# Sliding-window attention and token MLP, two layers: key-offset products summed in groups of 16, softmax pinned ahead of PV, one layer's norms shared between two engines

## The chip, the core and the metric

The kernel runs on one core of one Trainium2 chip. The core has TensorE (PE, matmuls), VectorE (DVE), ScalarE (ACT), GpSimd (POOL) and SyncE (SP, here only a queue that issues DMAs); each works through its own instruction queue, and semaphores tie the queues together. The metric is the device time of one execution in microseconds.

## The reference

Two attention layers and two token-mixing MLPs, applied in turn to x of 2048 tokens by 1024 features, all in bf16:

```python
for _ in range(2):
    x = x + A(layernorm(x))      # attention
    x = x + B(layernorm(x))      # MLP over tokens

def A(x):                        # 32 heads of 32
    q, k, v = split(x @ wqkv)
    # token s sees tokens s, s-2, ..., s-14 (8 offsets, dilation 2)
    logits = q[s] . k[s - 2w] / sqrt(32), w = 0..7; -1e9 where s - 2w < 0
    o = softmax(logits) weighted sum of v[s - 2w]
    return o @ wo

def B(x):
    h = layernorm(x)
    u = gelu(h.T @ w1 + b1)      # over tokens: 1024 x 2048 @ 2048 x 3584
    return (u @ w2 + b2).T
```

## The kernel before

**Two classes.** Because the dilation is 2, even and odd tokens never meet in the attention. The kernel treats them as two classes c = 0 and 1 of 1024 tokens each. Within a class, eight neighbouring tokens form a window. Features lie on the partitions: a feature tile `dt` is 128 features (4 heads), and four feature tiles make one unit n of the attention: n = 0 and 1 are class 0, n = 2 and 3 class 1.

**QK** (`qk`, L436 to L449). For each feature tile and each parity `par` of the key offset, DVE multiplies q with four shifted copies of k in one instruction of 128 x 4096 elements into a buffer T (L444). Two buffers of tag "T" are shared by T, by the PV products `pr` and by a copy of w2. TensorE then sums the 32 features of each head: eight matmuls (L449) with a 0/1 matrix `sel` of 128 x 32 columns, one for each of the eight token blocks, into a PSUM tile `sc`. The eight use four column strips of the array. Half a feature tile (one `par`) is thus one DVE instruction and one group of eight matmuls.

**Softmax** (`softmax_front` L453, `softmax_back` L463). ACT copies `sc` to L (L455), DVE finds and subtracts the maximum (L456 to L460), ACT takes the exp (L461), DVE sums, takes the reciprocal and multiplies into Pb (L466 to L470). POOL's queue writes Pb to DRAM (pd, L473) and reads it back, spread over the partitions of each head, as two halves pb (L487); there are two pb buffers, one for each half.

**PV** (`pv`, L489 to L511). For each feature tile and half `hf`, DVE multiplies pb with shifted v (two L505), adds the eight offsets in three steps (L509 twice, L511) and writes oT.

**Output projection** (`out_proj`, L611). oT times wo (L631) per token tile i and half n of the columns, plus the residual on DVE (L652, with the row sums, or L655), then a layer norm to h2. With the flag `on_act` the norm runs on ACT (L219 to L233: sums, square, Ln, Exp, scale), otherwise on DVE (bn_stats L202, L204, and L228) with Ln and Exp on ACT. Class 0 takes ACT for all eight tiles in both layers; class 1 alternates, and multiplies six of the eight feature tiles of its first three token tiles early.

**MLP.** `gemm1` (L682) multiplies h2 with w1 into g, 14 blocks of g; for the first 12 blocks class 0's part is computed ahead of time ("partials") and class 1's added later (L693, L694). `gemm2_tile` (L706) multiplies g with w2, adds bias and residual on DVE (L711), stores, normalises to `hb` and transposes by DMA to hT, the input of the next layer's projections (`project`, L412).

**What sets the order.** The attention's generator `stream` (L514) is the lead. Each step yields its engine, its planned cost, what it waits for, what it makes ready, and a lag. `weave` (L755) keeps one planned clock for PE and one for DVE, and while the lead would leave PE waiting it pulls PE work from the fills: the second class's tiles, v projections ahead, class 0's output projection ("out0") and partials. "out0" is also pulled when DVE has planned more than OUT0_GAP of work and PE is less than AHEAD in front of DVE. The order in which instructions are recorded gives a priority, and a scheduler of the language then orders each engine's queue by its own costs. It may put instructions of PV between those of the softmax, and split or merge neighbouring groups. Only the first tiles of layer 0 are written out by hand.

**Buffers that the change touches.** g_raw is 14 tiles of SBUF that hold g; the first six are also the landing place of x, the last eight that of class 1's v. PSUM has six banks for `ps` and two for `sc`. The pool "wb" has five buffers for wv, wo, w1 and w2 pieces, "x2" four for residual rows and `hb`.

Of the kernel before, what the change touches and what calls it, by code (L numbers as in the profile page):

```python
# [11 lines left out]
ALU = mybir.AluOpType  # L12
FP32 = mybir.dt.float32
BF16 = mybir.dt.bfloat16

P = 128
H = 32
DH = 32
W = 8
# [7 lines left out]
def kernel(  # L27
# [39 lines left out]
    PB_LAG = 12.0  # L67
    PDW = 4 * SB * W * TB + 512
    OUT0_GAP = 7.0
    AHEAD = 10.0  # L70
    assert D == H * DH and W == 8 and SC == 1024 and HD * KD == H and SB * CH == 32
    scale = float(DH) ** -0.5

# [7 lines left out]
    pers = pool("pers", 1)  # L81
    wqp = pool("wqp", 3)
    wbp = pool("wbp", 5)
    tpl = pool("tpl", 2)
# [6 lines left out]
    class at:  # L91
# [8 lines left out]
        def __exit__(self, *a):  # L100
            self.c[0] = tc.cur_priority
            tc.cur_priority = self.old

    tc.cur_priority = 10_000_000
    top = [1_000_000]
# [30 lines left out]
    sel = const.tile([P, SB * DQ, 32], BF16, name="sel")  # L136
# [28 lines left out]
    L = pers.tile([P, W, TB], FP32, name="L")  # L165
    m4 = pers.tile([P, 4, TB], FP32, name="m4")
    Pb = pers.tile([P, W, TB], BF16, name="Pb")
    g_raw = [pers.tile([P, 2 * KW if n >= NFB - KD else GF * D], BF16, name=f"g{n}") for n in range(NFB)]
    g = [t[:, 0:GF * D].rearrange("p (f d) -> p f d", d=D) for t in g_raw]
    v_g = [t[:].rearrange("p (r k) -> p r k", k=KW) for t in g_raw[NFB - KD:]]  # L170
# [181 lines left out]
    class Attn:  # L352

        def __init__(self, li, hT, early):
            self.li, self.hT, self.early = li, hT, early
            self.oT = [[None] * KD for _ in range(DIL)]
            self.wts = {}
            self.pbs = {}

        def v_of(self, c, dt):  # L360
            return v_g[dt] if c else v_t[dt % 2]
# [72 lines left out]
        def qk(self, n, dq):  # L434
            c, dt = n // NCQ, (n % NCQ) * DQ + dq
            if dq == 0:  # L436
                self.sc = pssp.tile([P, 2, 4, TB], FP32, name="sc", tag="sc")
            q, k = self.q_of(c, dt), self.k_of(c, dt)
            for par in range(2):
                yield "dve", 2.2, [("ready", 0, dt), ("ready", 1, dt)], [("free", x, dt % 2) for x in range(2)] if par and not self.apart(c, dt) else [], 0.0, 0.6 * bool(n)  # L440
                if n == 0:
                    yield "pe", 0.6, [], [], 0.0
                T = tpl.tile([P, 4, SC], BF16, name="T", tag="T")
                nc.vector.tensor_tensor(out=T[:], in0=q.unsqueeze(1).to_broadcast([P, 4, SC]),  # L444
                                        in1=window(k, par, 2, [(2, 4), (1, SC)]), op=ALU.mult)
                for sb in range(SB):
                    for gr in range(4):
                        b = SB * gr + sb
                        nc.tensor.matmul(self.sc[32 * gr:32 * gr + 32, par], lhsT=sel[:, sb * DQ + dq, :],  # L449
                                         rhs=T[:, :, b * TB:(b + 1) * TB],  # L450
                                         start=(dq == 0 and sb == 0), stop=(dq == DQ - 1 and sb == SB - 1))

        def softmax_front(self):  # L453
            yield "dve", 4.5, [], ["exp"], 1.2, 0.0
# [8 lines left out]
        def softmax_back(self, n):  # L463
            yield "dve", 3.0, ["exp"], [("pb", n, 0)], PB_LAG, 0.0
            yield "dve", 0.0, [], [("pb", n, 1)], PB_LAG + 6.0, 0.0
            nc.vector.tensor_tensor(out=m4[:], in0=L[:, 0:4, :], in1=L[:, 4:8, :], op=ALU.add)  # L466
            nc.vector.tensor_tensor(out=m4[:, 0:2, :], in0=m4[:, 0:2, :], in1=m4[:, 2:4, :], op=ALU.add)
            nc.vector.tensor_tensor(out=m4[:, 0, :], in0=m4[:, 0, :], in1=m4[:, 1, :], op=ALU.add)
            nc.vector.reciprocal(out=m4[:, 1, :], in_=m4[:, 0, :])
            nc.vector.tensor_tensor(out=Pb[:], in0=L[:], in1=m4[:, 1:2, :].to_broadcast([P, W, TB]), op=ALU.mult)  # L470
            base = self.pd(n)[0, 0]
            dst = bass.AP(base.tensor, base.offset, [(W * TB, 4 * SB), (PDW, CH), (1, W * TB)])
            nc.gpsimd.dma_start(out=dst, in_=Pb[:].rearrange("p u t -> p (u t)"))  # L473
            self.spread(n)
# [14 lines left out]
        def pv(self, n, half, hf, dqs=(0, 1)):  # L489


            c = n // NCQ
            for dq in (2 * half + x for x in dqs):
                dt = (n % NCQ) * DQ + dq
                if hf == 0 and c and dt < 2 * DIL:
                    self.oT[c][dt] = v_t[dt // 2][:, dt % 2, PADK + 8:PADK + 8 + SC]
                elif hf == 0:
                    self.oT[c][dt] = otp.tile([P, SC], BF16, name="oT", tag="oT")[:]
                waits = [("pb", n, hf)] + ([] if c else [("ready", 2, dt)])
                yield "dve", 4.7, waits, [("free", 2, dt % 2), "oT", ("oT", half)] if hf else [], 0.0, 0.0  # L500
                pb = self.pbs[(n, hf)]
                pr = tpl.tile([P, 4, W, TB], BF16, name="pr", tag="T")
                for par in range(2):
                    u = slice(4 * par, 4 * par + 4)
                    nc.vector.tensor_tensor(out=pr[:, :, u, :], in0=pb[:, :, u, :],  # L505
                                            in1=window(self.v_of(c, dt), par, 2 + hf * HT, [(TB, 4), (2, 4), (1, TB)]),
                                            op=ALU.mult)
                for wd in (4, 2):
                    nc.vector.tensor_tensor(out=pr[:, :, 0:wd, :], in0=pr[:, :, 0:wd, :], in1=pr[:, :, wd:2 * wd, :],  # L509
                                            op=ALU.add)  # L510
                nc.vector.tensor_tensor(out=self.oT[c][dt][:, hf * HT:(hf + 1) * HT].rearrange("p (b t) -> p b t", t=TB),  # L511
                                        in0=pr[:, :, 0, :], in1=pr[:, :, 1, :], op=ALU.add)
# [95 lines left out]
                nc.sync.dma_start(out=self.tiles[-1][:], in_=src)  # L608
            return self.tiles.pop(0)

    def out_proj(at_, c, res, dst, h2, on_act):  # L611

        early = 0 if on_act else 3
        if early:
            yield "pe", 1.28 * early * NDC, [("oT", 0), ("less", "oT", -12.0)], [], 0.0
        dst_v = rows(dst)
# [10 lines left out]
        def multiply(i, n, kts):  # L627
            if (i, n) not in banks:
                banks[(i, n)] = bank()
            for kt in kts:  # L630
                nc.tensor.matmul(banks[(i, n)][:], lhsT=at_.oT[c][kt][:, i * P:(i + 1) * P],  # L631
                                 rhs=wo_t[n][kt // 4][:, kt % 4, :], start=(kt == 0), stop=(kt == KD - 1))

        def kts(i):
            return range(KD - 2 if i < early else 0, KD)

        for i in range(early):
            for n in range(NDC):
                multiply(i, n, range(KD - 2))
        xrs = Rows([res[i] for i in range(NT)], 2)  # L640
        for i in range(NT):
            if early:
                yield "pe", 0.43 * len(kts(i)), ["oT"], [], 3.6
                on_act = i % 2 == 0
            xn = xrs.take()
            s1 = st("s1", [P, NDC]) if on_act else None
            for n in range(NDC):
                cols = slice(n * 512, (n + 1) * 512)
                multiply(i, n, kts(i))
                ps = banks.pop((i, n))  # L650
                if on_act:
                    nc.vector.scalar_tensor_tensor(out=xn[:, cols], in0=ps[:], scalar=1.0, in1=xn[:, cols], op0=ALU.mult,  # L652
                                                   op1=ALU.add, accum_out=s1[:, n:n + 1])
                else:
                    nc.vector.tensor_tensor(out=xn[:, cols], in0=ps[:], in1=xn[:, cols], op=ALU.add)  # L655
            nc.gpsimd.dma_start(out=dst_v[i], in_=xn[:])
# [167 lines left out]
    for li in range(2):  # L824
# [96 lines left out]
```

## Time and profile before

| | us |
|---|---|
| median of 3 runs | 1294.18 (1294.08 to 1295.04) |
| the profiled execution | 1291.79 |
| its span in the trace | 1290.0 |
| PE busy | 1263.8 (98%) |
| DVE busy | 680.5 (53%) |
| ACT busy | 502.7 (39%) |
| L449, `sel` matmuls, x512 | 38.5 |
| L444, T, x64 | 144.5 |
| L505, PV products, x128 | 152.2 |

The table's engine and line figures are those of the one profiled execution. Matmuls overlap in the array, so the busy time of PE's groups is a sum of overlapping durations within the group's line and not the time that they hold the array; a stretch of PE is read from its starts. "Idle before" and "waited for" name what ended a pause. TensorE's granted clock is full throughout. Layer 0's attention runs to about 304 us, its MLP to about 560, layer 1's attention to about 925, and the rest is the last MLP.

### The profile page before, as it was taken

The page shows a single profiled execution, that of the slowest core. Times are in us where ns is not written, and L with a number is a line of the kernel's source. Part 1 is how long each engine was busy: PE and PEld are TensorE (multiplying, and loading weights), DVE is VectorE, ACT ScalarE, POOL GpSimd, SP SyncE. Part 2 cuts the span into 40 slices and gives each one's busy share as a digit, 9 for nine tenths or more (in the row PEclk, how much of TensorE's full clock was granted, in tenths as well). Part 3 has the DMA queues.
Part 4 walks back from the last instruction along what each step waited for, and adds up shares of the span by engine and source line. Part 5 has one row for each costly group of instructions (what it writes and reads, how often), then busy time and mean ns, then how long its engine had stood idle before and what let it go on. Part 6 is the DMA issues. An engine that isn't in the chain of part 4 may idle for free. (4 is left out here: it accounts for less than half of the span.)

```text
span 1290.0 us, 15498 instructions
## 1 busy us (share of the span) xinstructions
PE 1263.8 (98%) x6163; PEld 574.5 (45%) x6284; DVE 680.5 (53%) x861; ACT 502.7 (39%) x836; POOL 60.8 (5%) x166
## 2 busy tenths in 40 slices
PE   8999999999999999999999999999999999999999
PEld 4344444444444444444444444444444444444444
DVE  6879899989013422335895734978920233011011
ACT  6845446635324533325414435484343344000000
POOL 3000001001000000000000000010000000000000
PEclk9999999999999999999999999999999999999999
DMA  9852436563422289953646652349252222334331
GB/s 253 188 122 87 118 106 167 163 153 109 136 82 82 61 221 301 298 147 94 153 125 179 164 135 84 72 142 226 67 179 76 72 82 73 121 121 136 103 112 53
DMA packets 217817, 173.01 MB, mean 134 GB/s; under 512 B 32080, under 2 KB 198352, under 8 KB 215696
## 3 DMA queue, kind: packets, MB, share of 16 engines
q1 hardware_dynamic: 206768, 126.11, 36.5%
q0 software_dynamic: 9248, 37.51, 10.3%
q10 hardware_dynamic: 1728, 8.39, 1.7%
q8 instruction: 49, 0.80, 0.3%
q14 instruction: 24, 0.20, 0.0%
HBM read 139.47 MB, written 26.21 MB: 128 GB/s over the span
## 5 line engine op out<-in xcount | busy, mean ns | idle before, releaser
L682 PE MATMUL ps<-h,w 128*128 128x512 bf16 x1756 | 386.7, 379 | 4.8 <-ACT h L233 2.1
L706 PE MATMUL ps<-g,w 128*128 128x512 bf16 (+1 forms) x1785 | 388.0, 376 | 3.4 <-ACT v L419 1.6
L706 PEld LDWEIGHTS <-w 128*128 128x128 bf16 x1820 | 177.4, 98 | 212.8 <-issue 6.0
L682 PEld LDWEIGHTS <-w 128*128 128x128 bf16 x1792 | 175.1, 98 | 215.8 <-issue 4.5
L412 PE MATMUL ps<-hT,wq 128*128 128x512 bf16 (+1 forms) x1085 | 241.4, 374 | 3.6 <-DVE xr L711 0.9
L693 DVE TENSOR_TENSOR tmp<-ps,g 128x512 f32<-128x512 f32 x96 | 66.4, 692 | 211.3 <-PE ps L682 206.0
L444 DVE TENSOR_TENSOR T<-q,k 128x4096 bf16<-128x4096 bf16 x60 | 135.6, 2286 | 63.2 <-ACT q L416 52.5
L711 DVE SCALAR_TENSOR_TENSOR xr<-ps,b_sb,xr 128x512 bf16<-128x512 f32 (+1 forms) x65 | 45.6, 737 | 230.7 <-PE ps L706 188.7
L412 PEld LDWEIGHTS <-wq 128*128 128x128 bf16 x1112 | 108.3, 100 | 131.6 <-issue 13.4
L509 DVE TENSOR_TENSOR pr<-pr 128x2048 bf16<-128x2048 bf16 (+1 forms) x128 | 119.2, 946 | 0.2
L694 ACT ACTIVATE g<-tmp,b_sb 128x512 bf16<-128x512 f32 x96 | 69.3, 721 | 93.3 <-DVE tmp L693 92.9
L412 PE MATMUL ps<-hT,wv 128*128 128x512 bf16 x436 | 100.6, 380 | 1.0 <-issue 0.5
L631 PE MATMUL ps<-wo,oT 128*128 128x512 bf16 x377 | 89.1, 379 | 2.7 <-DMA wo<-in_A_wo_dram 2.4
L688 ACT CAST g<-ps 128x512 bf16<-128x512 f32 x96 | 55.1, 589 | 91.5 <-PE ps L682 85.8
L419 ACT CAST k<-ps 128x1024 bf16<-128x1024 f32 x60 | 60.7, 1015 | 72.6 <-PE ps L412 71.2
L505 DVE TENSOR_TENSOR pr<-pb,v 128x2048 bf16<-128x2048 bf16 x64 | 75.9, 1215 | 21.1 <-DMA pb<-pd 11.0
L505 DVE TENSOR_TENSOR pr<-pb,g 128x2048 bf16<-128x2048 bf16 x64 | 76.3, 1215 | 11.0 <-DMA pb<-pd 11.0
L412 PEld LDWEIGHTS <-wv 128*128 128x128 bf16 x448 | 48.6, 112 | 50.5 <-issue 7.2
L631 PEld LDWEIGHTS <-oT 128*128 128x128 bf16 x384 | 37.2, 98 | 48.7 <-issue 4.6
L416 ACT CAST q<-ps 128x512 bf16<-128x512 f32 x60 | 34.8, 583 | 47.4 <-PE ps L412 47.4
L419 ACT CAST g<-ps 128x1024 bf16<-128x1024 f32 x36 | 36.6, 1016 | 40.7 <-PE ps L412 40.7
L737 ACT COPY odd<-w 128x896 bf16<-128x896 bf16 x32 | 30.0, 938 | 56.0 <-DMA w<-in_B_w_dram 55.8
(91 smaller groups left out, 606.1 us busy)
## 6 DMA issues: line engine op xcount, KB each, us to landing
w<-in_B_w_dram SPq DMA_DIRECT2D x56, 512.0 KB, 4.3
w<-in_B_w_dram SPq DMA_DIRECT2D x64, 448.0 KB, 3.8
wq<-in_A_wqkv_dram SPq DMA_DIRECT2D x38, 512.0 KB, 4.1
pb<-pd POOLq DMA_DIRECT2D x16, 1024.0 KB, 10.0
wo<-in_A_wo_dram SPq DMA_DIRECT2D x16, 512.0 KB, 4.0
xa<-xr POOLq DMA_DIRECT2D x32, 256.0 KB, 3.4
xr<-xa SPq DMA_DIRECT2D x32, 256.0 KB, 3.6
wv<-in_A_wqkv_dram SPq DMA_DIRECT2D x14, 512.0 KB, 5.7
```

Of the source, the lines that this page charges most:

```text
L412: nc.tensor.matmul(ps[:, lo:hi], lhsT=cols, rhs=self.hT[c][hf][:, kt, lo:hi], start=(kt == 0), stop=(kt == KD - 1))
L419: nc.scalar.copy(out=window(buf, 0, PADK + hf * HT, [(KW + 1, 2), (1, HT)]), in_=ps[:].unsqueeze(1).to_broadcast([P, 2, HT]))
L444: nc.vector.tensor_tensor(out=T[:], in0=q.unsqueeze(1).to_broadcast([P, 4, SC]), in1=window(k, par, 2, [(2, 4), (1, SC)]), op=ALU.mult)
L505: nc.vector.tensor_tensor(out=pr[:, :, u, :], in0=pb[:, :, u, :], in1=window(self.v_of(c, dt), par, 2 + hf * HT, [(TB, 4), (2, 4), (1, TB) ...
L509: nc.vector.tensor_tensor(out=pr[:, :, 0:wd, :], in0=pr[:, :, 0:wd, :], in1=pr[:, :, wd:2 * wd, :], op=ALU.add)
L631: nc.tensor.matmul(banks[(i, n)][:], lhsT=at_.oT[c][kt][:, i * P:(i + 1) * P], rhs=wo_t[n][kt // 4][:, kt % 4, :], start=(kt == 0), stop=( ...
L682: nc.tensor.matmul(ps[:], lhsT=wt[c][:, i, fl * P:(fl + 1) * P], rhs=h2[c][i // 4][:, i % 4, dc * 512:(dc + 1) * 512], start=(k == 0), sto ...
L688: nc.scalar.copy(out=gs, in_=ps[:])
L693: nc.vector.tensor_tensor(out=tmp[:], in0=ps[:], in1=gs, op=ALU.add)
L694: nc.scalar.activation(out=gs, in_=tmp[:], func=ACT.Gelu_apprx_tanh, bias=b1_sb[:, ft:ft + 1])
L706: nc.tensor.matmul(ps[:, 0:xc.stop - xc.start], lhsT=w2t(ft, c), rhs=g[ft // GF][:, ft % GF, xc], start=(ft == 0), stop=(ft == FT - 1))
L711: nc.vector.scalar_tensor_tensor(out=xo[:, xc], in0=ps[:, 0:xc.stop - xc.start], scalar=b2_sb[:, i, c:c + 1], in1=xo[:, xc], op0=ALU.add, ...
```

## The change

- `qk`: except in layer 0's n = 0, both T of a feature tile are made first and then summed in one group of 16 matmuls. A dependency of the first of the 16 on the second multiply, and a chain through the 16, keep the group together. The plan's step is 4.5 of DVE and then 1.1 of PE, where it was twice 2.2 and 0.6.
- `t_buf`: for layer 0's n = 1 and 2, T lies in g's first six tiles, which are now three double tiles `g_two`; elsewhere T keeps the two shared buffers.
- `self.prior`: each QK multiply, in the joined steps, is ordered behind the one before it or behind the last Pb, and each PV product is ordered behind the last QK multiply or Pb recorded before it, by dependencies of order on the same engine. So the softmax's DVE instructions up to Pb stand ahead of the PV products that are recorded after it.
- `out_proj`: `early` and `every` take the place of `on_act`. Class 0 keeps ACT for all tiles in layer 0 and alternates ACT and DVE in layer 1. Without `early`, the first column half of tiles 0 and 1 is multiplied before the rest.
- AHEAD is 5.0 instead of 10.0.

```diff
-    AHEAD = 10.0
+    AHEAD = 5.0
...
+    def follow(inst, other, how):
+        tc.add_manual_dep(inst.ins, other.ins.name, mybir.DependencyInfo(how, mybir.DependencyReason.DATA), reason="follow")
...
-    g_raw = [pers.tile([P, 2 * KW if n >= NFB - KD else GF * D], BF16, name=f"g{n}") for n in range(NFB)]
+    g_two = [pers.tile([P, 2 * GF * D], BF16, name=f"gg{n}") for n in range((NFB - KD) // 2)]
+    g_raw = [t[:, h * GF * D:(h + 1) * GF * D] for t in g_two for h in range(2)]
+    g_raw += [pers.tile([P, 2 * KW], BF16, name=f"g{n}")[:] for n in range(NFB - KD, NFB)]
...
+            ready = [("ready", 0, dt), ("ready", 1, dt)]
+            free = [] if self.apart(c, dt) else [("free", x, dt % 2) for x in range(2)]
+            joined = n > 0 or self.li > 0
+            if joined:
+                yield "dve", 4.5, ready, free, 0.0, 1.1
+            Ts = []
             for par in range(2):
-                yield "dve", 2.2, [("ready", 0, dt), ("ready", 1, dt)], [("free", x, dt % 2) for x in range(2)] if par and not self.apart(c, dt) else [], 0.0, 0.6 * bool(n)
-                if n == 0:
+                if not joined:
+                    yield "dve", 2.2, ready, free if par else [], 0.0, 0.0
                     yield "pe", 0.6, [], [], 0.0
-                T = tpl.tile([P, 4, SC], BF16, name="T", tag="T")
-                nc.vector.tensor_tensor(out=T[:], in0=q.unsqueeze(1).to_broadcast([P, 4, SC]),
-                                        in1=window(k, par, 2, [(2, 4), (1, SC)]), op=ALU.mult)
-                for sb in range(SB):
-                    for gr in range(4):
-                        b = SB * gr + sb
-                        nc.tensor.matmul(self.sc[32 * gr:32 * gr + 32, par], lhsT=sel[:, sb * DQ + dq, :],
-                                         rhs=T[:, :, b * TB:(b + 1) * TB],
-                                         start=(dq == 0 and sb == 0), stop=(dq == DQ - 1 and sb == SB - 1))
+                T = self.t_buf(n, dq, par)
+                mult = nc.vector.tensor_tensor(out=T, in0=q.unsqueeze(1).to_broadcast([P, 4, SC]),
+                                               in1=window(k, par, 2, [(2, 4), (1, SC)]), op=ALU.mult)
+                Ts.append(T)
+                if joined and self.prior:
+                    follow(mult, self.prior, mybir.DependencyClass.NoSync)
+                self.prior = mult
+                if not joined:
+                    self.qk_sum(dq, par, T)
+            if joined:
+                mms = self.qk_sum(dq, 0, Ts[0]) + self.qk_sum(dq, 1, Ts[1])
+                follow(mms[0], mult, mybir.DependencyClass.Sync)
+                for x, y in zip(mms[1:], mms):
+                    follow(x, y, mybir.DependencyClass.NoSync)
+
+        def t_buf(self, n, dq, par):
+            if self.li == 0 and 0 < n < 3:
+                return g_two[(2 * (n * DQ + dq) + par) % len(g_two)][:].rearrange("p (u t) -> p u t", u=4)
+            return tpl.tile([P, 4, SC], BF16, name="T", tag="T")[:]
...
-            nc.vector.tensor_tensor(out=Pb[:], in0=L[:], in1=m4[:, 1:2, :].to_broadcast([P, W, TB]), op=ALU.mult)
+            self.prior = nc.vector.tensor_tensor(out=Pb[:], in0=L[:], in1=m4[:, 1:2, :].to_broadcast([P, W, TB]),
+                                                 op=ALU.mult)
...
-                    nc.vector.tensor_tensor(out=pr[:, :, u, :], in0=pb[:, :, u, :],
-                                            in1=window(self.v_of(c, dt), par, 2 + hf * HT, [(TB, 4), (2, 4), (1, TB)]),
-                                            op=ALU.mult)
+                    mult = nc.vector.tensor_tensor(out=pr[:, :, u, :], in0=pb[:, :, u, :],
+                                                   in1=window(self.v_of(c, dt), par, 2 + hf * HT, [(TB, 4), (2, 4), (1, TB)]),
+                                                   op=ALU.mult)
+                    follow(mult, self.prior, mybir.DependencyClass.NoSync)
...
-    def out_proj(at_, c, res, dst, h2, on_act):
-
-        early = 0 if on_act else 3
+    def out_proj(at_, c, res, dst, h2, early=0, every=1):
+
...
+        if not early:
+            for i in range(2):
+                multiply(i, 0, range(KD))
         for i in range(NT):
             if early:
                 yield "pe", 0.43 * len(kts(i)), ["oT"], [], 3.6
-                on_act = i % 2 == 0
+            on_act = i % every == 0
...
-                multiply(i, n, kts(i))
+                if early or (i, n) not in banks:
+                    multiply(i, n, kts(i))
...
-        lead = chain(at_.stream(opening() if first else None), out_proj(at_, 1, res[1], xa[li][1], h2, on_act=False))
+        lead = chain(at_.stream(opening() if first else None), out_proj(at_, 1, res[1], xa[li][1], h2, early=3, every=2))
...
-                     "out0": out_proj(at_, 0, res[0], xa[li][0], h2, on_act=True),
+                     "out0": out_proj(at_, 0, res[0], xa[li][0], h2, every=li + 1),
```

More of the change, by code (lines that the diff above doesn't have):

```diff
@@ L167 @@
     Pb = pers.tile([P, W, TB], BF16, name="Pb")
-    g_raw = [pers.tile([P, 2 * KW if n >= NFB - KD else GF * D], BF16, name=f"g{n}") for n in range(NFB)]
+    g_two = [pers.tile([P, 2 * GF * D], BF16, name=f"gg{n}") for n in range((NFB - KD) // 2)]
+    g_raw = [t[:, h * GF * D:(h + 1) * GF * D] for t in g_two for h in range(2)]
+    g_raw += [pers.tile([P, 2 * KW], BF16, name=f"g{n}")[:] for n in range(NFB - KD, NFB)]
     g = [t[:, 0:GF * D].rearrange("p (f d) -> p f d", d=D) for t in g_raw]
-    v_g = [t[:].rearrange("p (r k) -> p r k", k=KW) for t in g_raw[NFB - KD:]]
+    v_g = [t.rearrange("p (r k) -> p r k", k=KW) for t in g_raw[NFB - KD:]]
     xa = [[dram.tile([SC, D], BF16, name=f"xa{li}{c}") for c in range(DIL)] for li in range(2)]
@@ L358, in __init__ @@
             self.pbs = {}
+            self.prior = None
         def v_of(self, c, dt):
@@ new lines, in t_buf, with qk_sum @@
+        def t_buf(self, n, dq, par):
+            if self.li == 0 and 0 < n < 3:
+                return g_two[(2 * (n * DQ + dq) + par) % len(g_two)][:].rearrange("p (u t) -> p u t", u=4)
+            return tpl.tile([P, 4, SC], BF16, name="T", tag="T")[:]
+        def qk_sum(self, dq, par, T):
+            mms = []
+            for sb in range(SB):
+                for gr in range(4):
+                    b = SB * gr + sb
+                    mms.append(nc.tensor.matmul(self.sc[32 * gr:32 * gr + 32, par], lhsT=sel[:, sb * DQ + dq, :],
+                                                rhs=T[:, :, b * TB:(b + 1) * TB],
+                                                start=(dq == 0 and sb == 0), stop=(dq == DQ - 1 and sb == SB - 1)))
+            return mms
```

## The prediction

> **What bounds the kernel now.** I read the page's busy times first, then the list of TensorE's own waits, then the timelines of PE and VectorE (DVE) around those waits and around the small `sel` matmuls (L449).
>
> ```profile
> span 1290.0 us, 15498 instructions
> ## 1 busy us (share of the span) xinstructions
> PE 1263.8 (98%) x6163; PEld 574.5 (45%) x6284; DVE 680.5 (53%) x861; ACT 502.7 (39%) x836; POOL 60.8 (5%) x166
> ```
>
> ```profile
> PE sc L449 <- DVE T L444: 3.6, 3, 1.9
> PE ps L631 <- DMA wo<-in_A_wo_dram: 2.4, 2, 1.7
> PE ps L682 <- ACT h L233: 2.1, 3, 1.0
> PE ps L706 <- ACT v L419: 1.6, 2, 0.9
> PE ps L412 <- DVE xr L711: 0.9, 1, 0.9
> ```
>
> TensorE is the bound from end to end; nothing else comes near. A change can pay in two ways only: less PE time, or fewer pauses of PE. In the PE timeline the pauses after the first 60 us are 1.85 (at 104.9, T), 1.71 (191.1, wo), 0.72 (244.8, h), 0.29 (629.6, wq), 0.92 (674.4, xr), 0.87 and 0.72 (710.3 and 711.4, v), 0.26 (754.7, hT), 0.65 (842.1, wo), 1.04 and 0.36 (873.1 and 880.3, h) and 0.81 us (948.2, w): 10.2 us in all, 4.3 in layer 0 and 5.9 in layer 1. That is the most that better ordering can give.
>
> The other source is the small matmuls. PE's timeline in layer 1:
>
> ```profile
> 765.19 0.62 PE L449 MATMUL sc<-T,sel 128*32 128x512 bf16 x8
> 765.74 1.92 PE L412 MATMUL ps<-hT,wv 128*128 128x512 bf16 x8
> 767.59 0.62 PE L449 MATMUL sc<-T,sel 128*32 128x512 bf16 x8
> 768.14 0.41 PE L412 MATMUL ps<-hT,wv 128*128 128x512 bf16 x1
> 768.48 0.62 PE L449 MATMUL sc<-T,sel 128*32 128x512 bf16 x8
> ...
> 849.96 0.61 PE L449 MATMUL sc<-T,sel 128*32 128x512 bf16 x8
> 850.51 3.63 PE L631 MATMUL ps<-wo,oT 128*128 128x512 bf16 x16
> 854.06 1.05 PE L449 MATMUL sc<-T,sel 128*32 128x512 bf16 x16
> 855.04 2.12 PE L631 MATMUL ps<-wo,oT 128*128 128x512 bf16 x8
> 857.13 0.61 PE L449 MATMUL sc<-T,sel 128*32 128x512 bf16 x8
> ```
>
> The first column is the start. A full matmul in a long run takes 0.216 us (128 of L631 from 917.89 to 945.52). Eight `sel` matmuls use four column strips side by side, so they stream as two: 0.432. From 765.19 to 767.59 are 2.40 us, of which a group of 8 and 8 full matmuls explain 0.432 + 1.727 = 2.16: 0.24 is lost. From 767.59 to 768.48, 0.89 - 0.432 - 0.216 = 0.24. The group of 16 at 854.06 (with the 9 full ones that the program has behind it; the trace lost one record) loses 3.07 - 0.863 - 1.943 = 0.26; the group of 8 at 849.96 0.21. So the loss belongs to the group, not to its size: 0.24 us, between 0.21 and 0.26.
>
> [...] the `v` casts stood behind `hb` L215, which waited 5.49 us at 686.69, and DVE then waited 6.60 us for `v`. [...] Here xb<-xr, issued behind two pb loads, took 10.61 us against a median of 4.2.
>
> **The change, part by part.**
>
> *Groups of 16.* In the programs' instruction order PE visits the `sel` groups 56 times before and 35 times after (the first eight, layer 0 n = 0, stay halves). 21 x 0.24 = **-5.0 us** (21 x 0.21 to 0.26: 4.4 to 5.5). All of it is on PE, which bounds, so nothing hides the gain. Matmul counts are the same.
>
> *The wait that it adds.* The group waits for both T. Behind it on PE stand the projections, GEMM pieces, everything. DVE's price is two T at 2.29:
>
> ```profile
> L444 DVE TENSOR_TENSOR T<-q,k 128x4096 bf16<-128x4096 bf16 x60 | 135.6, 2286 | 63.2 <-ACT q L416 52.5
> ```
>
> ```profile
> 760.74 4.49 DVE L444 TENSOR_TENSOR T<-q,k 128x4096 bf16<-128x4096 bf16 x2 [9.35 <-ACT q L416]
> 765.92 4.63 DVE L444 TENSOR_TENSOR T<-q,k 128x4096 bf16<-128x4096 bf16 x2 [0.69 <-PE sc L449]
> ```
>
> With two T buffers the next pair starts when the first half of the group has read its T: 0.73 us after the group's start (765.19 to 765.92). After the change the second group of a pair can start 0.73 + 4.49 + 0.1 = 5.32 us after the first. PE has 0.98 + 18 x 0.216 + 0.1 = 4.97 us of work there: 0.33 us short. That spacing of 18 occurs six times in layer 1: **+2.0**. In layer 0, n = 1 and 2 borrow g buffers (three pairs), which takes away DVE's waits for T buffers (0.23, 3.54, 0.26). Summing DVE's durations against PE's along both orders I get waits of 0.2 to 0.4 at about seven groups: **+2.0** in place of 1.85. Bounds: none at all, or a whole extra DVE instruction at each (see the rivals).
>
> *Softmax ahead of PV.* On DVE the exp gap is no longer filled in layer 0: 1.2 us each (1.18 at 605.17, where nothing fills it), four times, 4.8 us. Against that DVE loses the 4.0 of T waits, some 3 of the 7.03 us wait for pb at 82.8 (Pb is out 3 us sooner) and the 6.25 at 268.8: Pb to pb took 12.9 us (255.9 to 268.8), and three PV blocks of 4.34 = 13.0 now lie behind Pb. POOL's second pb load now waits for PV to free its buffer, and xa or xb stores queue behind it; the stores of two more tiles now go ahead of it. Net, DVE ends layer 0's attention some 4 us earlier, while 24 matmuls (5.2 us) more of the partial GEMM stand ahead of the second output projection. Its cover grows; no charge. In layer 1, xr L711 pairs move into the exp gap or ahead of PV: the pauses for xr and v (0.92 + 0.87 + 0.72 = 2.5) came from L711 standing behind PV and from xb behind pb. I leave 0.8: **-1.7** (0 to 2.5).
>
> *Output projection of class 0.* Both tiles' first columns come first, so the last wo piece is needed at the 21st matmul, not the 13th: 8 x 0.216 = 1.73 us later. 0.65 goes; of 1.71 I leave 0.5, since PE also gets there sooner: **-1.9** (1 to 2.4). In layer 0 the h pause (0.72) goes, because the last L652 stand ahead of T6 and T7 now: **-0.7**. In layer 1 four of eight norms move to DVE. From the last group's start the DVE order sums to 7.7 us up to tile 6's second L652, then ACT needs 4.4 to 5, with the exp put ahead of its L233: h ready at 12.8, wanted at 0.98 + 0.1 + 39 x 0.216 + 10 x 0.216 = 11.7. Tile 7's DVE norm is ready at 19.7, wanted at 18.6 + 1.1. So 1.1 in place of 1.40: **-0.3** (-1.4 to +2). ACT is relieved by about 16 us; DVE gets 4 x 1.9, and its last oT comes at 68 us after that group, PE's need at 70: covered by 2 us.
>
> *Left:* wq, hT and w pauses (1.4), the start and the last 60 us: no change.
>
> Sum: -5.0 (groups) + 2.0 (T, layer 1) + 0.15 (T, layer 0) - 1.7 - 1.9 - 0.7 - 0.3 = **-7.4 us**. The profiled execution took 1291.79 (span 1290.0 and 1.8 around it): 1284.4. The median of the runs, 1294.18, is 2.4 above it: **1286.8**.
>
> **Rivals.** (1) The pauses only change place, each order having its own: the joins alone, -5.0, 1289.2. For it: PE's pauses are short and have seven different causes. (2) Most pauses go: some 3 of 10.2 us stay, -12.2, 1282.0. For it: DVE is under half busy in much of layer 1. Against: the T shortage of 0.33 is in the program. (3) Slower: DVE is late at the second group of each pair where T has two buffers (ten places: layer 0 n = 3 and layer 1) by one more instruction of 1.1 us, such as a PV multiply ahead of T: 10 x 1.1 = 11, so +3.6, 1297.8. It decides from 7.4 / 10 = 0.74 us each. Against: in layer 1 DVE waits 9 and 13 us for q ahead of such pairs; for it: layer 0 is 20.0 of 20 us busy on DVE from 200 to 260. That the groups aren't joined at all is excluded by the instruction order.
>
> **Chances.** Forecast 0.52 (own range 1284.5 to 1289), joins alone 0.24, most pauses gone 0.14, slower 0.06, and 0.04 for a tie. The bounds of the parts make the forecast 1281 to 1292; I take 1281.0 to 1292.0. What a measurement can tell from no change is about 0.2%, 2.6 us: faster 0.87, same 0.08, slower 0.05.
>
> **What would show it.** In the new profile: groups of L449 x16, some 0.24 us less PE time each; PE's wait for T near 4 us in many short pieces; no wait for wo over 0.6; no PE wait of 1.85; DVE's exp gaps of 1.2 in layer 0. Wrong: PE waits for T above 10 us in sum, a wait at L631 for oT, or h L228 or L233 pauses over 3 us.

## The result and the profile after

The changed kernel took 1280.76 us (median of four runs, 1280.15 to 1281.44) where the kernel before took 1294.61 beside it (1294.08 to 1295.36): 13.9 us less by the medians; the ratio estimated from all the runs is 0.9896, 95% interval 0.9881 to 0.9910. The forecast was 1286.8; the time lies 0.2 us below the range's low end. The profiled execution took 1280.6 us, 11.2 less than that of the kernel before, so about 2.7 us of the gain are not a difference of the two profiles at all. They have a cause of their own, found below (e5 and the last section).

The page of the kernel after, its first lines:

```profile
span 1278.8 us, 15455 instructions
## 1 busy us (share of the span) xinstructions
PE 1258.0 (98%) x6163; PEld 577.4 (45%) x6284; DVE 689.9 (54%) x869; ACT 489.3 (38%) x812; POOL 61.3 (5%) x166
```

TensorE is still the bound. DVE got 9.4 us of work more and ACT 13.4 less: layer 1's norms moved as planned. TensorE's own waits in the kernel after (total, times, longest):

```profile
PE sc L480 <- DVE T L456: 3.4, 9, 1.2
PE ps L719 <- ACT h L238: 2.0, 2, 1.2
...
PE ps L664 <- DVE oT L545: 0.7, 1, 0.7
```

The lines for wo, v, xr, hT, wq and w are gone; T waits are many and short, the longest (1.2) in the first 60 us; one wait for oT is new. Summed from PE's timeline after the first 60 us, the pauses over 0.2 us are 5.3 us where they were 10.2. The joined groups, from PE's timeline in layer 1:

```profile
758.50 1.05 PE L480 MATMUL sc<-T,sel 128*32 128x512 bf16 x16
759.48 3.64 PE L418 MATMUL ps<-hT,wv 128*128 128x512 bf16 x15
...
763.77 1.05 PE L480 MATMUL sc<-T,sel 128*32 128x512 bf16 x16 [0.22 <-DVE T L456]
```

The two groups stand 5.27 us apart (the forecast had 5.32), and the second waits 0.22: the small new wait that the prediction priced at 0.33.

### The profile page after: what moved, and what is told of

It is laid out like the page before. It is cut to its first block, busy times and chain, and to the rows that moved or that the text cites. A ratio compares the mean times of both kernels' runs of the same rounds, so it can differ in the third digit from the quotient of the medians.

```text
span 1278.8 us, 15455 instructions
## 1 busy us (share of the span) xinstructions
PE 1258.0 (98%) x6163; PEld 577.4 (45%) x6284; DVE 689.9 (54%) x869; ACT 489.3 (38%) x812; POOL 61.3 (5%) x166
## 4 chain that ended last, share of the span: by engine, by line
PE 76%; DVE 5%; issue 2%; ACT 1%; DMA 0%; DVEq 0%
PE ps L719 30%; PE ps L743 29%; PE ps L418 11%; PE ps L664 4%; DVE T L456 2%; PE sc L480 1%; DVE pr L538 1%; DVE pr L543 1%; DVE xr L689 0%; ACT h L227 0%; ACT h L238 0%; DMA wo<-in_A_wo_dram 0%; DVE v L545 0%; DVE xr L692 0%; ACT ln L200 0%
## 5 line engine op out<-in xcount | busy, mean ns | idle before, releaser
L719 PE MATMUL ps<-h,w 128*128 128x512 bf16 x1754 | 385.6, 379 | 4.0 <-ACT h L238 2.0
L719 PEld LDWEIGHTS <-w 128*128 128x128 bf16 x1792 | 175.2, 98 | 214.1 <-issue 3.4
L743 PE MATMUL ps<-g,w 128*128 128x512 bf16 (+1 forms) x1017 | 225.9, 376 | 1.2 <-issue 0.2
L743 PE MATMUL ps<-gg,w 128*128 128x512 bf16 (+1 forms) x766 | 170.9, 376 | 0.9 <-issue 0.2
L456 DVE TENSOR_TENSOR T<-q,k 128x4096 bf16<-128x4096 bf16 x44 | 99.0, 2284 | 70.5 <-ACT q L422 52.4
L730 DVE TENSOR_TENSOR tmp<-ps,gg 128x512 f32<-128x512 f32 x48 | 33.2, 692 | 150.2 <-PE ps L719 148.2
L730 DVE TENSOR_TENSOR tmp<-ps,g 128x512 f32<-128x512 f32 x48 | 33.2, 692 | 49.7 <-PE ps L719 46.9
L731 ACT ACTIVATE gg<-tmp,b_sb 128x512 bf16<-128x512 f32 x48 | 34.6, 721 | 49.9 <-DVE tmp L730 49.9
L731 ACT ACTIVATE g<-tmp,b_sb 128x512 bf16<-128x512 f32 x48 | 34.6, 721 | 43.5 <-DVE tmp L730 43.1
```

What stands on the lines that cost most here:

```text
L456: mult = nc.vector.tensor_tensor(out=T, in0=q.unsqueeze(1).to_broadcast([P, 4, SC]), in1=window(k, par, 2, [(2, 4), (1, SC)]), op=ALU.mult)
L719: nc.tensor.matmul(ps[:], lhsT=wt[c][:, i, fl * P:(fl + 1) * P], rhs=h2[c][i // 4][:, i % 4, dc * 512:(dc + 1) * 512], start=(k == 0), sto ...
L730: nc.vector.tensor_tensor(out=tmp[:], in0=ps[:], in1=gs, op=ALU.add)
L731: nc.scalar.activation(out=gs, in_=tmp[:], func=ACT.Gelu_apprx_tanh, bias=b1_sb[:, ft:ft + 1])
L743: nc.tensor.matmul(ps[:, 0:xc.stop - xc.start], lhsT=w2t(ft, c), rhs=g[ft // GF][:, ft % GF, xc], start=(ft == 0), stop=(ft == FT - 1))
```

## The experiments

The parts have short names here: the joins are the groups of 16, the pins the orders through `self.prior`, the columns and the norms the two edits of `out_proj`. Each ratio is against the kernel before, measured beside that run (its medians were 1295.31 for e1 to e4, 1293.52 for e6 to e9 and 1293.51 for e10 to e12). The changed kernel itself was not measured again beside them; e6 below, which is close to it, came out within 0.1 us of it. Beside each time stand three figures of its profile: the pauses of PE over 0.2 us after the first 60 us; the time lost to a halved TensorE clock, summed over slices of 2 us as (1 - granted clock) x 2, outside the pauses; and the rest of the span, which is mostly work. Gaps under 0.2 us are left with the work: nearly all of them stand right behind a group of `sel` matmuls in traces that lack some 121 of PE's 6284 matmul records, and none stands there in the traces that have all records (e5, e10, e11, e12), so they are taken for missing records.

| kernel | visits to `sel` | median us | ratio (95%) | pauses | half clock | rest |
|---|---|---|---|---|---|---|
| before, first profile | 56 | 1294.61 | | 10.2 | 0 | 1279.8 |
| before, again (e5) | 56 | 1296.38, one execution | | 11.7 | 3.4 | 1279.5 |
| columns alone (e11) | 56 | 1292.46 | 0.9994 (0.9986 to 1.0002) | 9.8 | 1.7 | 1279.9 |
| pins alone (e4) | 57 | 1293.68 | 0.9988 (0.9982 to 0.9995) | 9.8 | 1.7 | 1279.9 |
| joins alone (e1) | 35 | 1291.63 | 0.9971 (0.9959 to 0.9982) | 14.4 | 0 | 1275.7 |
| **after** | 35 | 1280.76 | 0.9896 (0.9881 to 0.9910) | 5.3 | 0 | 1273.5 |
| after, visit added (e3) | 63 | 1287.81 | 0.9941 (0.9928 to 0.9953) | 5.2 | 0 | 1281.0 |
| after, columns as before (e6) | 35 | 1280.84 | 0.9900 (0.9884 to 0.9915) | 4.9 | 0 | 1273.9 |
| after, norms on ACT (e7) | 35 | 1281.34 | 0.9902 (0.9888 to 0.9915) | 5.3 | 0 | 1273.9 |
| after, two T buffers (e8) | 35 | 1285.98 | 0.9936 (0.9924 to 0.9949) | 9.4 | 0 | 1274.7 |
| after, no pins (e9) | 35 | 1297.57 | 1.0029 (1.0021 to 1.0037) | 17.5 | 1.7 | 1274.5 |
| after, AHEAD 10 (e10) | 35 | 1286.20 | 0.9945 (0.9933 to 0.9957) | 9.2 | 0 | 1274.4 |
| after, more T buffers (e12) | 35 | 1279.12 | 0.9889 (0.9876 to 0.9902) | 3.8 | 0 | 1273.2 |
| after, halves (e2) | 54 | 1297.82 | 1.0025 (1.0009 to 1.0041) | 17.4 | 3.6 | 1278.5 |

Read the last column first: it is 1278.5 to 1279.9 with 54 to 57 visits, 1281.0 with 63, and 1273.2 to 1275.7 with 35. Nearly all else that the parts do is in the two columns before it. Where a part's worth is given below as a difference from the changed kernel's median, the two profiled executions give much the same (7.3 for 7.1 in e3, 15.0 for 16.8 in e9, 5.3 for 5.2 in e8, 4.8 for 5.4 in e10, 1.9 for 1.6 in e12).

**e3, the price of a visit.** In each of the 28 joined groups a full-width matmul of 64 columns by a matrix of zeros stands after the fourth `sel` matmul, so it adds zero to `sc` and splits one visit into two.

```diff
+                if more and sb == 0:
+                    mms.append(nc.tensor.matmul(self.sc[:, 0, 0, 0:64], lhsT=zero[:], rhs=ident[:, 0:64], start=False, stop=False))
```

> The changed kernel with one full-width matmul of 64 columns and zero weights put between the 4th and 5th sel matmul of each of the 28 joined groups (it adds zero to sc), so that PE visits the column strips 63 times instead of 35. Theory A: 28 x (0.24 + 0.03) = 7.6 us more, 1288.4. Rival B [...]: 1 to 2 us more, about 1282.

It took 7.05 us more than the changed kernel, 7.05 / 28 = 0.25 us for each added visit. PE's timeline of this kernel:

```profile
763.33 0.40 PE L482 MATMUL sc<-T,sel 128*32 128x512 bf16 x4
763.66 0.20 PE L486 MATMUL sc<-ident,zero 128*128 128x64 bf16 x1
763.80 0.83 PE L482 MATMUL sc<-T,sel 128*32 128x512 bf16 x12
764.56 3.64 PE L420 MATMUL ps<-hT,wv 128*128 128x512 bf16 x15
```

From 763.33 to 764.56 are 1.23 us; the whole group in the kernel after takes 0.98 (758.50 to 759.48). By an estimate from the prediction's 0.216 us for a matmul of 512 columns, the 64 columns themselves are 64 / 512 x 0.216 = 0.03 of the 0.25. Pauses stayed near 5.2, so the 7.05 us are not pauses: a visit cost 0.22 to 0.25 here, near the 0.24 of the prediction.

**e1, the joins alone** in the kernel before: two T buffers, no pins, AHEAD 10, old columns and norms.

```diff
-                yield "dve", 2.2, [("ready", 0, dt), ("ready", 1, dt)], ...
-                    yield "pe", 0.6, [], [], 0.0
+                yield "dve", 4.5, ready, free, 0.0, 1.1
...
+                mms = self.qk_sum(dq, 0, Ts[0]) + self.qk_sum(dq, 1, Ts[1])
```

> The kernel before with the joined groups alone (35 visits to the sel matmuls instead of 56); T keeps its two shared buffers, the softmax isn't pinned, output projection and AHEAD are as before. Theory A (each visit costs PE 0.24 us, whatever its size, and pauses of PE make the rest of the gain): 21 x 0.24 = 5.0 us less PE time, of which longer waits for T in layer 0 take back 1 to 3: 1290 to 1293 against 1294.6. Rival B (the joins' gain is eaten by PE waiting for both T, and the pinned softmax is what made the kernel faster): 1294 to 1298.

The median falls by 3.7 us (1291.63 against 1295.31), but the two profiles are the same: a span of 1290.1 against 1290.0. The rest fell by 4.1 us against the first profile, while pauses rose from 10.2 to 14.4. So the 3.7 are not the joins' saving on PE. All six runs of e1 have a granted clock of 1.000, and most executions of the kernel before beside it do not (see the last section); the 11 of these 35 that do have a median of 1292.9. PE's waits in this kernel:

```profile
PE sc L472 <- DVE T L453: 5.9, 15, 1.7
PE ps L706 <- ACT h L236: 3.5, 3, 1.4
PE ps L415 <- DVE xr L735: 2.2, 2, 1.3
PE ps L415 <- DMA hT<-hb: 1.8, 1, 1.8
```

So the first rival's "the pauses only change place" is what the joins do by themselves, and worse: they save on PE and give it back in waits for T, h, xr and hT. None of these pauses goes above 1.77 us after the first 60, and its six runs lie within 0.8 us, which matters below.

**e4, the pins alone, and e9, the changed kernel without them.** The edit of e4 adds `self.prior` with its two `follow` calls to the kernel before; e9 takes both out of the changed kernel:

```diff
-                if joined and self.prior:
-                    follow(mult, self.prior, mybir.DependencyClass.NoSync)
...
-                    follow(mult, self.prior, mybir.DependencyClass.NoSync)
```

> The kernel before with the pins alone: QK multiplies, Pb and PV products on DVE in recorded order, so the softmax is ahead of PV; halves of 8, two T buffers, AHEAD 10, output projection as before. Theory A: no PE time saved, pauses of PE for xr and v (2.5 us) and part of those for T and h shorter, DVE's exp gaps of 1.2 us covered: 1290 to 1293. Rival B: the pins are worth most of the 13.6 us: below 1287. A second rival: with two T buffers DVE can't fill its waits any more and falls behind: 1296 or more.

> The changed kernel without the orders between QK multiplies, Pb and PV products, so that the scheduler may mix the softmax into PV. Theory A: the pauses for xr, v and hT in layer 1 (1.0 to 1.8 us each, as in the kernel with joins alone) are back: 1284 to 1287. Rival B (AHEAD 5, the columns and the norms did that): within 1.5 us of 1280.8.

Alone, pins are worth 1.6 us by the medians, a little less than expected; they take away the xr and v pauses in layer 1 (2.3 to 2.5 us in both profiles of before, 0 in e4), but the last wo piece came later, with a wait of 3.70. Inside the changed kernel they are worth 1297.57 - 1280.76 = 16.8, far more than the 3 to 6 us expected: layer 1's pauses came back as thought (xr twice, v, hT), but layer 0's waits for T came with them, 9.4 us in sum. DVE's timeline of e9, in layer 0 where T lies in g's tiles (gg):

```profile
104.81 4.48 DVE L456 TENSOR_TENSOR gg<-q,k 128x4096 bf16<-128x4096 bf16 x2
109.22 2.35 DVE L536 TENSOR_TENSOR pr<-pb,v 128x2048 bf16<-128x2048 bf16 x2
111.49 2.28 DVE L456 TENSOR_TENSOR gg<-q,k 128x4096 bf16<-128x4096 bf16 x1
```

Two PV products stand between the two T of one feature tile (109.22 to 111.49; the first T is the second of the pair of instructions at 104.81). A group of 8 could have run on the first T; the group of 16 waits for both, and PE paused for 1.66 us until 113.8. At 107.1 and 151.4, with PV ahead of the T as well (and that PV itself held up 3.40 us by pb at 144.35), it paused for 2.90 and 2.92. This is rival 3's mechanism (PV multiplies ahead of a T), at full size. The pins are what excludes it, so joins and pins are one change: alone, they bring 3.7 and 1.6 us in the medians, and neither shortens the profile.

**e8, two T buffers.** Without the lines in `t_buf` that borrow g's tiles.

```diff
-            if self.li == 0 and 0 < n < 3:
-                return g_two[(2 * (n * DQ + dq) + par) % len(g_two)][:].rearrange("p (u t) -> p u t", u=4)
```

> The changed kernel with T in its two shared buffers everywhere: no borrowed g tiles in layer 0's n = 1 and 2. Theory A: DVE waits for T buffers (0.7 us and up at each second pair) and PE's second group of a pair is 0.3 to 1 us late, in five or six places: PE's wait for T grows by 2 to 4 us, 1283 to 1285. Rival B (DVE has room in layer 0 and the groups are spaced widely enough): within 1 us of 1280.8.

5.2 us slower than the changed kernel, where 2 to 4 were expected. PE's waits for T go from 3.4 us at 9 places to 7.1 at 16, among them 1.04 at 140.4 and 1.16 at 206.6, and the wait for oT from 0.67 to 1.43.

**e10, AHEAD back at 10.**

```diff
-    AHEAD = 5.0
+    AHEAD = 10.0
```

> The changed kernel with AHEAD 10 again. Theory A: AHEAD moves only where class 0's output projection is pulled in layer 1, and PE has work on both sides: within 1 us of 1280.8. Rival B: pulled too early it makes PE wait for wo or h: 1282.5 or more.

5.4 us slower, a miss: this part was thought to be worth less than 1 us. Up to the last group of layer 1 the two kernels run alike (PE reaches the partials, L719, at 859.87 and 860.07). Then, in e10, on PE and on DVE:

```profile
863.69 1.46 PE L719 MATMUL ps<-h,w 128*128 128x512 bf16 x6 [1.06 <-DVE xr L689]
...
868.30 4.31 PE L719 MATMUL ps<-h,w 128*128 128x512 bf16 x18 [1.42 <-DVE xr L692]
874.96 1.24 PE L719 MATMUL ps<-h,w 128*128 128x512 bf16 x5 [2.35 <-DVE h L233]
```

```profile
862.14 0.94 DVE L501 RECIPROCAL m<-m 128x128 f32<-128x128 f32 x1
863.00 0.62 DVE L689 SCALAR_TENSOR_TENSOR xr<-ps,xr 128x512 bf16<-128x512 f32 x1
```

The same residual on DVE in the kernel after:

```profile
855.96 0.63 DVE L689 SCALAR_TENSOR_TENSOR xr<-ps,xr 128x512 bf16<-128x512 f32 x1
...
857.68 0.69 DVE L689 SCALAR_TENSOR_TENSOR xr<-ps,xr 128x512 bf16<-128x512 f32 x1
```

In e10 tile 6's residual (L689) stands behind nearly the whole softmax, at 863.00. In the kernel after, DVE does it at 855.96 and 857.68, among the steps of the maximum. PE's pauses there are 5.1 us in e10 and 0.85 in the kernel after. AHEAD only tells the plan when to take a tile of the first class's projection, and with it the place of that tile's residual in DVE's queue.

**e11, the column order alone, and e6, the changed kernel without it.** e11 adds these lines to the kernel before (with a test that leaves out later what they have done), and e6 takes them from the kernel after:

```diff
+        if not early:
+            for i in range(2):
+                multiply(i, 0, range(KD))
```

> The kernel before with the columns of the output projection in the new order, and nothing else; SP's queue still has two wq loads ahead of the last wo load. Theory A (the unprofiled runs of the kernel before are 2 to 3 us slower than its profile, and scatter, because the wait for wo at 191 us varies and the clock sinks after it): with the piece wanted 1.7 us later the median falls by more than the 1.7 + 0.65 us of the profile's two waits, to 1290 to 1291.5, and the runs scatter by less than 2 us. Rival B (another pause or the load on the chip makes the scatter): the median falls by 2 or less, and the scatter stays at 4 us or more.

> The changed kernel with class 0's output projection tile by tile again, so that wo's second column half is wanted 8 matmuls (1.7 us) sooner. Theory A (the wait for wo in layer 0 went because SP's queue now has three wo loads ahead of the two wq loads, whichever column comes first): only layer 1's 0.65 us is back, 1281 to 1282. Rival B (the columns' order is what covers the load): waits for wo of 1.7 and 0.65 us and more, 1283.5 or more.

In e11 the waits for wo are 0.49 in layer 0 and none in layer 1, as the forecast's sum had it; but its time is 0.9994 of before's, an interval that holds 1, and its runs still spread over 4.0 us, so the column order is not the cause of the spread. In e6 the wo wait of layer 0 stays away all the same; only 0.59 in layer 1 comes back, and the time is the same. What took away the wait of 1.71 is on SP's queue. The kernel before, then e6:

```profile
165.53 1.40 SPq L621 DMA_DIRECT2D wo<-in_A_wo_dram  x2
177.53 7.28 SPq L390 DMA_DIRECT2D wq<-in_A_wqkv_dram  x2
185.31 0.55 SPq L621 DMA_DIRECT2D wo<-in_A_wo_dram  x1
```

```profile
164.77 3.37 SPq L654 DMA_DIRECT2D wo<-in_A_wo_dram  x3
...
176.45 7.28 SPq L396 DMA_DIRECT2D wq<-in_A_wqkv_dram  x2
```

Before, the last wo piece stands behind two wq loads that hold the queue from 177.53 until 185.31. Now all the wo pieces are issued ahead of these. The joins alone (e1) have the new order, pins and columns alone the old one: joining the groups changed the plan, and with it the place of these loads. e6 shows that the columns are not what took the wait away; that the order of the loads is what did is read from the queues, and no run changed that order alone.

**e7, layer 1's norms of class 0 all on ACT** (`every=1`).

```diff
-                     "out0": out_proj(at_, 0, res[0], xa[li][0], h2, every=li + 1),
+                     "out0": out_proj(at_, 0, res[0], xa[li][0], h2, every=1),
```

> The changed kernel with all eight norms of layer 1's class 0 on ACT again. Theory A (the norms' share is worth little, since 42 matmuls cover the last tile): PE's wait for h in layer 1 grows from 0.85 to 1.5 or 2: 1281.3 to 1282. Rival B (ACT's chain was what held the partial GEMM and the copies behind it): 1284 or more. Rival C (DVE, relieved of 8 us, does better): 1279.5.

The pause for h that ends at 865.3 is 1.82 us in place of 0.85. The median is 0.6 higher, less than the intervals can tell apart; the pause is what shows it.

**e2, groups of eight again** in the changed kernel, pins and the rest kept.

```diff
-                yield "dve", 4.5, ready, free, 0.0, 1.1
+                yield "dve", 2.2, [("ready", 0, dt), ("ready", 1, dt)], ...
+                    yield "pe", 0.6, [], [], 0.0
```

> The changed kernel with the sums of a feature tile in halves of 8 again (54 visits instead of 35), all else kept: pins, borrowed T buffers, columns first, shared norms, AHEAD 5. Theory A: 19 x 0.24 = 4.6 us more than the changed kernel's 1280.8, so 1285.4, and some pauses more or less (1284 to 1287). Rival B: within 1.5 us of 1280.8.

1297.82 us (1293.01 to 1302.38), ratio 1.0025 (1.0009 to 1.0041). It isn't a clean undo. The plan moved, and PE waited 6.73 us for wv at 135.5 and 4.63 for wo at 202.1: wv was issued at 123.59, just ahead of pb loads of 1 MB at 123.70 and 129.36, and landed at 135.4. So its time says nothing on the price of a visit; e3 does. It shows only that in this plan with halves the other parts gained nothing.

**e5, the kernel before once more**, unchanged.

> The kernel before once more, one look. If its runs scatter because of the wait for wo in layer 0, this profile's time and that wait move together against the first profile's 1291.8 and 1.71 us, and a longer wait shows a lower granted clock behind it.

1296.38 us, where its first profile had 1291.79. Two pauses account for most of it: T at 104.9 took 2.05 in place of 1.85, wo at 193.2 took 2.08 in place of 1.71, and after each the granted TensorE clock was 0.50 for some 3.4 us. The stretches after the T pause, in e5 and in the first profile (window, length, busy us and instructions of PE, PEld, DVE, ACT and POOL, granted clock, DMA share, GB/s):

```profile
106.00:108.00 2.00, 2.00 (x6) 0.76 (x5) 2.00 (x2) 0.00 (x0) 0.00 (x0) 0.50 0.20 71
108.00:110.00 2.00, 2.00 (x13) 0.42 (x12) 1.33 (x2) 1.02 (x1) 0.00 (x0) 0.71 0.03 8
```

```profile
106.00:108.00 2.00, 2.00 (x15) 0.67 (x13) 2.00 (x2) 0.64 (x1) 0.00 (x0) 1.00 0.10 35
```

Six matmuls run from 106 to 108 where 15 did; eight of the 15 are a `sel` group that in e5 starts only at 109.19, where it started at 107.47. Each drop takes 0.50 x 3.41 = 1.7 us of work away. Together 2 x 1.7 + 0.6 (the two pauses longer) + 1.4 (a wq wait of 1.66 in place of 0.29) = 5.4, less 0.5 for shorter waits elsewhere: 4.9, where the two executions are 4.6 apart.

**e12, T in g's free tiles in layer 1 too**, for the second class's units, as its first six tiles are free there as well.

```diff
-            if self.li == 0 and 0 < n < 3:
+            if (self.li == 0 and 0 < n < 3) or (self.li == 1 and n > 1):
```

> The changed kernel with the borrowed T buffers also in layer 1's n = 2 and 3, where g is free. Theory A: PE's waits for T there (0.22 three times and 0.5) go: 0.7 to 1.2 us less than 1280.8. Rival B: the same, since PE then waits for h or w.

1279.12 us (1278.73 to 1279.89), 1.6 less than the changed kernel and the fastest here. The two were not measured side by side, but their runs don't overlap, and the trace shows the cause: the four T waits from 763.8 to 850.7 (0.22 three times and 0.50: 1.16) are gone.

## Why the prediction was off

The direction and the first term were right. The sum in the profile was -7.4 and is -11.2 (6.3 of work, 4.9 of pauses), and a further 2.2 us lie in the last step. Point by point:

- **Groups, -5.0: right.** 0.25 per visit in e3, 21 times that is 5.3. (Eight `sel` matmuls more in one group took 0.98 - 0.55 = 0.43 us in the prediction's timeline, 854.06 to 855.04 and 849.96 to 850.51; it reckoned 0.432.) The rest of the span fell by 6.3 from the first profile, and by 3.8 to 6.7 in any pair of kernels with 56 or 57 and 35 visits; of the 1.3 beyond the 5.0, 0.4 are shorter waits in the first 60 us, and the rest is open.
- **T in layer 1, +2.0: right.** Six pauses of 0.22 to 0.25 are there, 1.4 in all, and one of 0.50 at 850.7: 1.9. (The prediction's own figures give 5.32 - 4.97 = 0.35 for each, not 0.33.) e12 confirms their cause, the buffers, by taking four of them away.
- **T in layer 0, "waits of 0.2 to 0.4 at about seven groups: +2.0": failed.** One wait of 0.30 is left, so this term was 1.7 too high. What the borrowed buffers do was mis-sized: e8, without them, has seven such waits, 3.4 us in sum. Setting DVE's durations against PE's along both orders charged DVE with shortages that three pairs of buffers even out.
- **xr and v, -1.7: short by 0.8.** All 2.5 went, and the pins did it (e4 has none of these pauses either; e1 and e9 have them).
- **wo, -1.9: nearly the size, -2.4, but by luck: in layer 0 by another mechanism.** Columns first would have left 0.5, as e11 measured (0.49). With SP's new order 0 is left in layer 0, and the columns take away layer 1's 0.6 (e6). The prediction followed the matmuls to their loads, and not the loads to their new place in SP's queue.
- **Layer 0's h, -0.7: failed.** A pause of 1.17 at 230.8 stands there instead, for the h of one norm on ACT (L238, from 229.49). PE enters the partials at 227.94, in one piece, where before it entered at 232.62 with three groups among them.
- **A wait for oT, named as a sign against the forecast: present, but 0.67 us.** DVE did Pb (179.09) and then PV, whose oT ended at 188.07; PE reached the projection at 182.97, 3.0 us earlier than before. The pause is there only in kernels with pins (not in e1 or e9; with pins alone, e4, PE waited there for wo instead), so it goes with the softmax ahead of PV, and that term had no charge for it.
- **Layer 1's h, -0.3: right, 0.85 left where 1.1 was forecast.** e7 shows that the norms on DVE are worth 1.0 of pause.
- **The 1.4 of wq, hT and w, left unchanged: 0.4 remain**, in a gap at 746.3 for which the trace names no cause.
- **AHEAD: the step that is missing.** The prediction doesn't cost it. It is worth 5.4 us in the changed kernel (e10).
- **"The median of the runs, 1294.18, is 2.4 above it": failed as a constant.** It was added to the new profile, whose own kernel has its median 0.2 above its profile. The 2.4 belongs to the kernel before: 44 of its 78 executions have a mean granted clock below 1.000, and the other 34 have a median 0.9 us above its first profile (the last section has the figures). That this profile was one without a drop was luck, and the prediction took the distance for a constant.

The misses in the profile (-1.3 -0.1 -1.7 -0.8 -0.5 +1.2 +0.7 -0.2 -1.0) sum to -3.7 of the -3.8 found; with the -2.2 of the last step they are the 6.0 us between 1286.8 and 1280.76. The mechanism of the second rival, "Most pauses go", came nearer, though 5.3 us of pauses stay and not 3.

How far the parts depend on each other is the larger finding. Taking away pins, AHEAD or the borrowed buffers from the changed kernel costs 16.8, 5.4 and 5.2 us; that sum of 27 is twice the whole gain. Added to the kernel before, the pins bring 1.6 and the joins 3.7, and none of this in the profile. A sum of parts, each costed against the trace of before, did not give these figures.

What stays open: why the last parts of AHEAD's plan moved tile 6's residual. Only the order of the instructions was seen, not the scheduler's reason.

## What to carry to other kernels

Price an edit of an order in two sums, PE's work and PE's pauses: the first can be worked out ahead of the run (here 6.3 us against a forecast 5.0), the second, as far as this case shows, only for the whole change at once, since one queue's order decided which wait was left (SP's for the wo wait of 1.71, DVE's for the 5.1 us of pauses in e10). Before adding the distance from a profiled execution to the median, look for what makes it: here pauses of PE of 2.05 and 2.08 us (e5) were each followed by a drop of the clock worth 1.7 us more, and the changed kernel's four executions all have a mean granted clock of 1.000. And when two halves of a wait are joined, see to it that nothing can stand between the two producers; in this kernel that order was worth more than the joining.

## What the runs showed of the hardware that was not expected

- **TensorE's clock was halved at some pauses near 2 us and above.** Pauses of 1.96 (e11), 2.05 and 2.08 (e5), 2.90 (e9), 3.70 (e4), 4.63 and 6.73 us (e2) each went with a granted clock of 0.50 for 3.41 or 6.83 us, and none up to 1.89 us did; but two longer ones, 2.92 (e9, at 151.4) and 2.35 us (e10, at 875.0), left it at 1.00. One drop of 3.41 us at 0.50 takes away 0.50 x 3.41 = 1.7 us of work.
- **The length of a pause did not tell the cases apart.** e9 has both, with pauses of 2.90 and 2.92 us that end at 107.1 and 151.4. In slices of 2 us its clock falls at 108.5. Here are the 3.41 us ahead of the drop and those of the drop, then, twelve times 3.41 us later, the same two stretches for the other pause (window, length, busy us and instructions of PE, PEld, DVE, ACT and POOL, granted clock, DMA share, GB/s):

```profile
105.08:108.49 3.41, 1.34 (x17) 0.59 (x19) 3.41 (x2) 0.27 (x1) 0.00 (x0) 1.00 0.79 267
108.49:111.90 3.41, 3.27 (x9) 1.06 (x7) 3.41 (x4) 0.42 (x1) 0.00 (x0) 0.50 0.01 4
...
149.45:152.87 3.42, 1.45 (x18) 0.63 (x20) 3.42 (x3) 0.05 (x1) 0.00 (x0) 1.00 0.01 2
152.87:156.28 3.41, 3.41 (x17) 1.52 (x17) 3.41 (x6) 1.29 (x2) 0.00 (x0) 1.00 0.00 0
```

  PE is idle for 3.41 - 1.34 = 2.07 us ahead of the drop, and for 3.42 - 1.45 = 1.97 in the stretch with no drop after it; 1.00 of the other pause lies ahead of that stretch. Ahead of all seven drops (two in e2, two in e5, one each in e4, e9 and e11) PE was idle for 1.96 to 2.75 us of 3.41. (In e2's long pauses the next stretches, with 3.41 and 2.41 us idle, were at 0.50 too, and so were the 3.41 us after each.) In the traces without a drop no 3.41 us between 60 and 1230 us have more than 1.85 us idle, except at e10's pause of 2.35. In e5 both long pauses lie whole within the 3.41 us ahead of its drops, at 105.7 and 194.5; these start 88.8 us apart and e2's two 68.2, which is close to 26 and 20 times 3.41. That the place of a pause in such steps decides with its length is an estimate from these figures; no run moved a pause to test it.
- **It shows as scatter.** The record has each execution's mean granted clock. Of the 78 of the kernel before that were measured beside e1 to e12, 34 have 1.000, with a median of 1292.7 us, 32 have 0.999 (1294.9), 8 have 0.998 (1296.0) and 4 have 0.997 (1296.8). So some 0.9 of the 2.4 us between the first profile (1291.79) and the median are there at a clock of 1.000 too, and the rest goes with the clock. All 33 executions of the changed kernel, e1, e3, e6, e7, e8 and e12 have 1.000; of e10 two in five have less, of e11 4 in 14, of e4 20 in 22, of e9 18 in 20, of e2 all 13. The first group spreads by 0.6 to 2.1 us from run to run, the second by 2.4 to 9.4, though from more runs, which widens a range by itself.
- **The visit's price was nearly the same for two ways of making it**: 0.24 from the halves of before; 0.25 from a full-width matmul of 64 columns put inside a group (e3), of which the columns themselves are, by the estimate there, 0.03.
